# The last unit's values as 64-row products in two PSUM banks, in a transformer block on one core

## The chip, the cores and the metric

One NeuronCore of a Trainium2 chip. The metric is the device time of one execution in microseconds (us); the kernel before took 1579.61 us, the median of three runs (1579.14, 1579.61, 1584.3).

## What is computed

```
xn  = layernorm(x)                                   # x: 2048 tokens x 512
q   = xn @ wq  (32 heads of 16);  k = xn @ wk, v = xn @ wv  (one head, shared)
o   = softmax(q k^T / 4) @ v                         # per head, 2048 x 2048
att = o @ wo
h   = xn @ w1 + b1;  act = h * tanh(softplus(h))     # 1792 wide
out = x + att + act @ w2
```

All inputs and the output are float32.

## The kernel before

The tokens are cut into 4 chunks of 512. A **unit** is 4 heads of one chunk, so there are 32 units, numbered 0 to 31; they run one after the other. In a unit PE makes, for each of 16 tiles of 128 keys and each of 4 heads, a score product (L509, `score`): 128 keys x 512 queries into one PSUM bank. ACT takes the exponential out of PSUM into a tile `pt`, of one bank (L945, 128x512) or of two neighbouring banks at once (L937, 128x1024). When all four heads of a key tile are there, `values` (L511 to L519; its matmul is L513) multiplies them with V: 128 keys x 32 columns, 16 of which are v and 16 ones, which give the softmax's denominators. Head h goes to the partitions 32h to 32h+31 of bank 7, and the 16 key tiles of a unit are added up there. I call the four products of one key tile **a V**. They are full float32, and each matmul leaves two records in the trace, so a V has 8. After the 16th V `attended` (L523) copies bank 7 with ACT to a tile `ov` (L525); for the units 0 to 30 it is stored and gathered back in another layout, for the last unit it stays.

Other products fill PE between scores: the hidden layer (`h..`), the second matrix (`y..`) and the attention's output (`f..`), all at L880. Scores, maxima and these fillers use 64 rows of the array: the upper or the lower half. I call the halves **lanes**; lane 0 is rows 0 to 63, lane 1 rows 64 to 127, and two products in the two lanes run side by side, in different banks. A filler product is split into a lane-0 and a lane-1 part that add into the same bank.

The order of all this is a string, `PLAN`, that is read letter by letter (from L978), and the digit behind a letter names the bank. What the letters in this case mean:

- `e`/`E`: a score in lane 0/1, then its exponential; `f`/`F`: the first score of a wide exponential, whose second score is the next `e` or `E` and takes the next bank. Digit: bank; then a digit or letter for the slot of `pt`.
- `h`/`H`: half a filler product in lane 0/1. The first half of a product is followed by its bank.
- `V`: the next V. `Z`: ACT (or DVE) empties a finished filler product out of its bank (L890 for `y`).
- `|`: PE drains. `G`, `O`, `Q`, `R`, `T` start loads or steps of the output's attention part.

Every engine runs its own instructions in this order, and an instruction waits by semaphore for what it reads and for its bank to be free. So PE's queue stands still behind a score whose bank ACT is still reading. Up to unit 30 the stage also takes the row maxima of the next unit (`s`/`S`, L450, read by DVE at L462); in unit 31 there is none, and DVE has nothing to do. The banks 0 to 6 hold scores and fillers, bank 7 the values.

Behind the last V stands `last_quotient` (L560 to L586). PE first makes 18 products of the output (`last_sums(0, 2)`, L595, with all 128 rows and columns). Then two products with a selection matrix `pick` take the denominators (`pd`, L569) and the values (`po`, L570) out of `ov` into the order that is needed. ACT takes a logarithm and an exponential of `pd` (L574, L575), DVE finishes the quotient (L576 to L578), it is split in two parts (L581, L582), while PE makes 18 more products (`last_sums(2, NT)`); the last 12 products need the quotient. DVE adds each 128-token result to what was there (L585) and SP stores it.

Of the kernel before, what the change touches and what calls it, by code (L numbers as in the profile page):

```python
# [17 lines left out]
P = 128  # L18
# [5 lines left out]
KT = S // P  # L24
KC = S // CT
HG = 4
NU = NC * H // HG
# [132 lines left out]
    "3HhHE6iHhhE2pHs4hOE5ohHHHhe6mS3s2ZVe4nS6E5gE3hNhhChS0e2ahE4bS6hhS5hhhE0eZS3VS6f4cEs2e3fE0mVh1e6aS2e4gS5E3nVE0bs6"  # L160
    "He2cHs3MHe4fHe5hs0HHHs6He2ks3VQF4is6eS0E2ls3Vs6Hf4oS0Es2Ve3aS6H0e4bhS5E2ihHHhs3e6kHS4he5dHhs2HE3chHHs6hRF4ehHes3"
    "S2ZVE6js3e4lE5gGS1hH2HhhHs6hE3hhHs4HE1mhe5nAHhHhS6hE3oZS4s1VHs6E3pf4aeHJE0ce1iTVAP6VVE3dF4eeH6hHHF0gheHHhhe3jHhH"
    "HhhF4kehGHhf0mEVZDVE3if4aeF0ohEGe2hhVVOH3e0gf4cEHe2aHhhCHhHf0ehHEHHHhhhZF4keVf0iH6EhhhhHhHE2bHf4mEHHhhF0ohheZE2h"
    "VVe4gF0ceE5af2eEVGVF0ieF4keVf2mGEH0HHe1bHhhhhhhZHF4oHef2cEVH1e6aHHHf4gEhhhf2eHHhEQhVE6ihf4kEZf2mEVVf4oEH6HHE0jhH"
    "hhhhhZHf2aHeGF4ceRVVF0eeF2ghhEf4kEVF0mehhhf2iEhZVVVTO"
)
PIECES = (
# [11 lines left out]
def attention_and_mlp(ctx: ExitStack, tc: tile.TileContext, x, wq, wk, wv, wo, w1, b1, w2, out):  # L179
    nc = tc.nc  # L180
    E = mybir.EngineType
    PE, SP = nc.tensor, nc.sync
    ACT, DVE, POOL = nc.scalar, nc.vector, nc.gpsimd
# [176 lines left out]
    V = const.tile([P, KT, 2 * DH], F32, name="V")  # L360
# [137 lines left out]
    PT = {}  # L498
# [11 lines left out]

    def values(u, kt):  # L511
        for h in range(HG):
            PE.matmul(  # L513
                BANK[7][h * 32 : (h + 1) * 32],
                V[:, kt],
                PT.pop((u * KT + kt) * HG + h),
                start=kt == 0,
                stop=kt == KT - 1,
            )  # L519

    OD, OHL = {}, {}

    def attended(u):  # L523
        ov = OV[u % 2]
        ACT.activation(ov, BANK[7], AF.Copy)  # L525
        if u == NU - 1:
            return
        j, g = divmod(u, 2)
        if g == 0:
            OD[j] = scratch.tile([2, P, CT], F32, tag="o", name=f"o{u}_dram", bufs=NU // 2)  # L530
        SP.dma_start(out=OD[j][g], in_=ov)
# [28 lines left out]
    def last_quotient():  # L560

        c, mt = NC - 1, DT - 1
        rows = slice(64, P)
        pick = late_pool.tile([P, 2, HG * DH], F32, name="pick")
        DVE.tensor_copy(pick.rearrange("p k (h d) -> p k h d", h=HG), ident.rearrange("p (h k d) -> p k h d", h=HG, k=2))
        po, pd = (BANK[4 + k][rows] for k in range(2))
        ov = OV[(NU - 1) % 2]
        last_sums(0, 2)
        PE.matmul(pd, pick[:, 1], ov, start=True, stop=True)  # L569
        PE.matmul(po, pick[:, 0], ov, start=True, stop=True)  # L570
        last_sums(2, NT)
        hi, lo = (OHL[c, mt][rows, k] for k in range(2))
        o, d, r, z = oc[rows], dc[rows], r0[rows], z0[rows]
        ACT.activation(z, pd, AF.Ln)  # L574
        ACT.activation(r, z, AF.Exp, scale=-1.0)  # L575
        DVE.tensor_tensor(out=d, in0=pd, in1=r, op=ALU.mult)  # L576
        DVE.scalar_tensor_tensor(out=r, in0=d, scalar=2.0, in1=r, op0=ALU.subtract, op1=ALU.mult)
        DVE.scalar_tensor_tensor(out=o, in0=po, scalar=-1.0, in1=r, op0=ALU.mult, op1=ALU.mult)  # L578
        for t in range(NT):
            q = slice(t * P, (t + 1) * P)  # L580
            ACT.activation(hi[:, q], o[:, q], AF.Copy)  # L581
            DVE.tensor_tensor(out=lo[:, q], in0=o[:, q], in1=hi[:, q].bitcast(F32), op=ALU.subtract)  # L582
        for t in range(NT):
            last_products(t, mt)
            DVE.tensor_tensor(out=YS[t], in0=BANK[t], in1=YS[t], op=ALU.add)  # L585
            SP.dma_start(out=of[c * CT + t * P : c * CT + (t + 1) * P, :], in_=YS[t])  # L586

    def last_sums(t0, t1):
        for t in range(t0, t1):
            for mt in range(DT - 1):  # L590
                last_products(t, mt)

    def last_products(t, mt):
        for k, (i, j) in enumerate(TERMS):
            PE.matmul(  # L595
                BANK[t],
                OHL[NC - 1, mt][:, i, t * P : (t + 1) * P],
                RG[(blocks_of[NC - 1, "wo"] + mt) % RING][:, j],
                start=mt == 0 and k == 0,
                stop=mt == DT - 1 and k == 2,  # L600
            )
# [228 lines left out]
    def tiles(n, shape, name, dtype=F32):  # L830
        return [late_pool.tile(shape, dtype, name=f"{name}{i}") for i in range(n)]

    banks = late_ps.tile([P, 8, CT], F32, name="banks")
    BANK = [banks[:, i] for i in range(8)]
# [5 lines left out]
    TY, OV = tiles(2, [P, D], "ty"), tiles(2, [P, CT], "ov")  # L840
# [60 lines left out]
    for p in todo + [None]:  # L901
        c, kind, i, t = (NC - 1, "f", 0, 0) if p is None else (p.c, p.kind, p.i, p.t)
# [74 lines left out]
    for token in word:  # L977
        k = count.get(token, 0)  # L978
# [10 lines left out]
        elif token == "|":  # L989
            PE.drain()  # L990
        elif token == "V":
            values(*divmod(k, KT))
        elif token == "P":
            sent[0] = place_maxima(k, bank=BANK[digit()])
        elif token == "D":
            sent[0]()
        elif token == "Z":
            ended.pop(0).end()
        elif token == "U":
            exponential(k)  # L1000
        elif token == "N":
            ACT.activation(tz, TN[k % 2], AF.Ln, bias=2.0)
        elif token == "M":
            inverse(k)
        elif token == "A":
            hidden_tile(k)
        elif token == "B":
            split_block()
        elif token == "K":
            store_block()  # L1010
        elif token == "W":
            request("w1", k % FT, WB[k % BLOCKS])
        elif token == "G":
            request(*blocks[k], RG[k % RING])
        elif token == "L":
            LOADS[k]()
        elif token == "X":
            reload(k)
        elif token == "J":
            SP.dma_start(**dict(zip(("out", "in_"), outgoing.pop(0))))  # L1020
        else:
            {"O": attended, "C": collect, "Q": logarithm, "R": divide, "T": attention}[token](k)
    last_quotient()


# [26 lines left out]
```

## Time and profile before

| | us |
|---|---|
| median of three runs | 1579.61 |
| the profiled execution | 1579.41 |
| its span, first to last instruction | 1577.3 |
| PE busy | 1554.8 (99%) |
| DVE busy | 1344.5 (85%) |
| ACT busy | 1343.3 (85%) |
| POOL busy | 862.6 (55%) |
| first V of unit 31 starts | 1529.75 |
| its last V is done, the tail's products start | 1560.23 |

Times inside the span count from the first instruction. A row of the timeline has the start, the length, the engine, the source line, the operation, output and inputs, the shape, and the number of instructions that it merges; in brackets the idle time ahead of it and what ended it. "64*128" is the part of the array that is used: 64 rows, 128 columns. A row that merges several is as long as from the first's start to the last's end.

### The profile page before, as it was taken

Reading aid. Unit: us, or ns where it says so; the run is one execution under the profiler, and the core shown is the slowest. Engines: PE = TensorE matmul, PEld = TensorE weight load, DVE = VectorE, ACT = ScalarE, POOL = GpSimd, SP = SyncE. Lnnn points to the kernel's source line nnn. Section 1 sums busy time; section 2 is a strip of 40 time slices with the busy share of each in tenths; the row PEclk is TensorE's granted clock in tenths of the full one; section 3 lists DMA queues with packets and bytes.
Section 4 is the critical chain, followed back from the end, with each engine's and each line's share of the span. In section 5 each row is a group of like instructions: output and inputs, shape, how many; then the busy total and the mean of one; then the engine's idle time right before and its main releaser. Section 6 shows DMA issues by size and latency. Waiting matters only on the chain.

```text
span 1577.3 us, 30275 instructions
## 1 busy us (share of the span) xinstructions
PE 1554.8 (99%) x11589; PEld 855.3 (54%) x11589; DVE 1344.5 (85%) x2215; ACT 1343.3 (85%) x2394; POOL 862.6 (55%) x749
## 2 busy tenths in 40 slices
PE   8989999999999999999999999999999999999999
PEld 6565554555555555555555555555555555555554
DVE  8819999898899889999898999898988898999841
ACT  5548988999899889898899898898888888888996
POOL 5845765587377455643365664452465563543652
PEclk9999999999999999999999999999999999999999
DMA  6682332123233212024223202223231212221130
GB/s 189 250 304 65 131 92 91 60 87 124 84 119 91 85 43 88 29 86 161 98 80 110 101 13 93 70 64 133 90 111 53 93 45 84 85 98 64 62 95 34
DMA packets 66966, 152.00 MB, mean 96 GB/s; under 512 B 9446, under 2 KB 19750, under 8 KB 66438
## 3 DMA queue, kind: packets, MB, share of 16 engines
q1 hardware_dynamic: 66758, 150.06, 28.4%
q8 instruction: 91, 1.49, 0.4%
q14 instruction: 53, 0.43, 0.1%
q10 hardware_dynamic: 64, 0.02, 0.0%
HBM read 97.98 MB, written 51.12 MB: 95 GB/s over the span
## 4 chain that ended last, share of the span: by engine, by line
PE 95%; DVE 2%; ACT 1%; DMA 1%; POOL 1%; issue 0%; SPq 0%; POOLq 0%; ACTq 0%; DVEq 0%
PE banks L513 32%; PE banks L880 23%; PE banks L509 18%; PE banks L450 17%; PE q L656 2%; DVE nm L467 1%; PE banks L595 1%; PE kv L372 0%; PE banks L481 0%; DVE st L304 0%; PE s L450 0%; DVE xs L326 0%; POOL q L412 0%; DMA QS<-mhl 0%; DMA w_dram<-wblk 0%
## 5 line engine op out<-in xcount | busy, mean ns | idle before, releaser
L462 DVE TENSOR_REDUCE nm<-banks 128x1 f32<-128x512 f32 x1984 | 1243.2, 683 | 160.0 <-PE banks L450 110.7
L945 ACT ACTIVATE pt<-banks 128x512 f32<-128x512 f32 x1608 | 867.3, 604 | 119.3 <-PE banks L509 52.7
L450 PE MATMUL banks<-KS,QS 48*128 48x512 f32 x1984 | 680.8, 422 | 6.5 <-ACT pt L945 5.7
L509 PE MATMUL banks<-QS,KS 64*128 64x512 f32 x2048 | 681.8, 419 | 1.1 <-DMA QS<-mhl 1.0
L513 PE MATMUL banks<-pt,V 128*32 128x512 f32 x4096 | 536.4, 603 | 0.0
L509 PEld LDWEIGHTS banks<-QS,KS 64*128 64x128 f32 x2048 | 329.9, 185 | 223.6 <-DVE nm L462 102.4
L450 PEld LDWEIGHTS banks<-KS,QS 48*128 48x128 f32 x1984 | 327.4, 185 | 203.6 <-DVE nm L462 97.7
L880 PE MATMUL banks<-X,wblk 64*128 64x512 f32 x1296 | 333.0, 398 | 0.3
L880 PE MATMUL banks<-ring,act 64*128 64x512 f32 x1344 | 333.1, 397 | 0.1
L937 ACT ACTIVATE pt<-banks 128x1024 f32<-128x1024 f32 x220 | 223.9, 1027 | 39.3 <-PE banks L509 28.3
L880 PEld LDWEIGHTS banks<-X,wblk 64*128 64x128 f32 x1296 | 214.6, 186 | 30.6 <-issue 10.7
L880 PEld LDWEIGHTS banks<-ring,act 64*128 64x128 f32 x1344 | 214.1, 185 | 31.5 <-issue 8.9
L891 POOL TENSOR_TENSOR ysb<-ysb,ty 128x512 f32<-128x512 f32 x80 | 102.7, 1284 | 177.3 <-ACT ty L890 177.2
L513 PEld LDWEIGHTS banks<-pt,V 128*32 128x32 f32 x4096 | 85.5, 108 | 171.4 <-issue 159.5
L636 POOL TENSOR_TENSOR tn<-tn,tr 128x512 f32<-128x512 f32 x54 | 69.5, 1288 | 176.2 <-ACT tr L955 176.0
L950 POOL TENSOR_SCALAR tu<-tu 128x512 f32<-128x512 f32 x54 | 80.2, 1486 | 96.1 <-ACT tu L949 96.0
L235 POOL TENSOR_TENSOR act<-th,act 128x512 fp32r<-128x512 f32 x56 | 72.0, 1287 | 104.6 <-ACT act L234 88.9
L639 POOL TENSOR_TENSOR th<-th,tn 128x512 f32<-128x512 f32 x56 | 72.1, 1288 | 0.0
L638 POOL TENSOR_TENSOR tz<-tz,tn 128x512 f32<-128x512 f32 x54 | 69.6, 1290 | 4.5
L952 POOL TENSOR_TENSOR tn<-tn,tu 128x512 f32<-128x512 f32 x54 | 69.5, 1287 | 4.5
L640 POOL TENSOR_TENSOR th<-th,tz 128x512 f32<-128x512 f32 x54 | 69.6, 1288 | 4.2
L880 PE MATMUL banks<-ring,ohl 64*128 64x512 f32 x288 | 64.5, 395 | 0.0
(113 smaller groups left out, 985.7 us busy)
## 6 DMA issues: line engine op xcount, KB each, us to landing
wblk<-w_dram SPq DMA_DIRECT2D x42, 512.0 KB
ring<-w_dram SPq DMA_DIRECT2D x42, 512.0 KB
QS<-q_dram SPq DMA_DIRECT2D x62, 192.0 KB
q_dram<-q SPq DMA_DIRECT2D x16, 512.0 KB
o_dram<-ov SPq DMA_DIRECT2D x31, 256.0 KB
raw_w<-in_B_w_dram SPq DMA_DIRECT2D x28, 256.0 KB
w_dram<-wblk SPq DMA_DIRECT2D x14, 512.0 KB
w_dram<-ring SPq DMA_DIRECT2D x14, 512.0 KB
```

The source lines that it names most:

```text
L235: POOL.tensor_tensor(out=lo, in0=src, in1=hi.bitcast(F32), op=ALU.subtract)
L450: PE.matmul(tile, QS[u][rows, pair, qt * P : (qt + 1) * P], KS[rows, kc * CT : (kc + 1) * CT], start=True, stop=True,)
L462: DVE.tensor_reduce(out=m[:, a : a + 1], in_=tile, axis=AX.X, op=ALU.max)
L509: PE.matmul(bank, KS[rows, kt * P : (kt + 1) * P], QS[u][rows, pair], start=True, stop=True)
L513: PE.matmul(BANK[7][h * 32 : (h + 1) * 32], V[:, kt], PT.pop((u * KT + kt) * HG + h), start=kt == 0, stop=kt == KT - 1,)
L638: POOL.tensor_tensor(out=z, in0=z, in1=n, op=ALU.subtract)
L639: POOL.tensor_tensor(out=h, in0=h, in1=n, op=ALU.mult)
L880: PE.matmul(self.p, w[rows], x[rows], start=self.first, stop=not any(self.todo))
L891: POOL.tensor_tensor(out=YS[t], in0=YS[t], in1=ty, op=ALU.add)
L937: ACT.activation(slots[slot // 2], banks[:, bank : bank + 2], AF.Exp, scale=SCALE)
L945: ACT.activation(PT[n], BANK[bank], AF.Exp, scale=SCALE)
L950: POOL.tensor_scalar_min(tu, tu, U_MAX)
```

## The change

In the last unit a V is made of eight products: for each head one of the upper 64 keys into bank 7 and one of the lower 64 keys into bank 6. Bank 6 is no longer there for scores and fillers from the first V of unit 31 on: the string's letters stay as they were, its bank digits are new, and one drain `|` is added. Bank 6 is copied by DVE to the other `ov`, and each of the two selecting sums becomes two products that add the two tiles.

```diff
-"...F4keVf0iH6EhhhhHhHE2bHf4mEHHhhF0ohheZE2h"
-"VVe4gF0ceE5af2eEVGVF0ieF4keVf2mGEH0HHe1bHhhhhhhhZHF4oHef2cEVH1e6aHHHf4gEhhhf2eHHhEQhVE6ihf4kEZf2mEVVf4oEH6HHE0jhH"
-"hhhhhZHf2aHeGF4ceRVVF0eeF2ghhEf4kEVF0mehhhf2iEhZVVVTO"
+"...F4keVf0iH2E|hhhhHhHE4bHf0mEHHhhF4ohheZE0"
+"hVVe1gF4ceE3af0eEVGVF4ieF0keVf4mGEH3HHe0bHhhhhhhhZHF4oHef0cEVH2e4aHHHf0gEhhhf4eHHhEQhVE0ihf4kEZf0mEVVf4oEH3HHE0jh"
+"HhhhhhZHf4aHeGF0ceRVVF4eeF0ghhEf4kEVF0mehhhf4iEhZVVVTO"
...
     def values(u, kt):
         for h in range(HG):
-            PE.matmul(
-                BANK[7][h * 32 : (h + 1) * 32],
-                V[:, kt],
-                PT.pop((u * KT + kt) * HG + h),
-                start=kt == 0,
-                stop=kt == KT - 1,
-            )
+            p = PT.pop((u * KT + kt) * HG + h)
+            for bank, rows in ((7, slice(0, P)),) if u + 1 < NU else ((7, slice(0, 64)), (6, slice(64, P))):
+                PE.matmul(
+                    BANK[bank][h * 32 : (h + 1) * 32], V[rows, kt], p[rows], start=kt == 0, stop=kt == KT - 1
+                )
...
         ACT.activation(ov, BANK[7], AF.Copy)
         if u == NU - 1:
+            DVE.tensor_copy(OV[(u + 1) % 2], BANK[6])
             return
...
-        ov = OV[(NU - 1) % 2]
         last_sums(0, 2)
-        PE.matmul(pd, pick[:, 1], ov, start=True, stop=True)
-        PE.matmul(po, pick[:, 0], ov, start=True, stop=True)
+        for out, k in ((pd, 1), (po, 0)):
+            for i in range(2):
+                PE.matmul(out, pick[:, k], OV[i], start=i == 0, stop=i == 1)
         last_sums(2, NT)
```

On PE at the first V of unit 31 (`F4keVf0iH...` in the string; L509 scores, L513 values, L880 a filler of the second matrix; "waits" names the engines whose semaphores the instruction waits for), before:

```order
L509 MATMUL banks<-QS_77,KS 128x512
L513 MATMUL banks<-pt_1112,V 32x512
L513 MATMUL banks<-pt_1119,V 32x512
L513 MATMUL banks<-pt_1115,V 32x512
L513 MATMUL banks<-pt_1119,V 32x512
L509 MATMUL banks<-QS_77,KS 128x512 [waits Activation_49]
L880 MATMUL banks<-ring_1120,act_1131 128x512 [waits DMAHW5_49,Activation_49]
```

and in the change, where lines behind L519 have moved and L515 is the matmul of `values`, L879 that of the fillers:

```order
L509 MATMUL banks<-QS_77,KS 128x512
L515 MATMUL banks<-pt_1112,V 32x512
L515 MATMUL banks<-pt_1112,V 32x512 [waits Activation_49]
L515 MATMUL banks<-pt_1119,V 32x512 x2
L515 MATMUL banks<-pt_1115,V 32x512 x2
L515 MATMUL banks<-pt_1119,V 32x512 x2
L509 MATMUL banks<-QS_77,KS 128x512
L879 MATMUL banks<-ring_1120,act_1131 128x512 [waits DMAHW5_49]
```

Each of the four products has become two, and the wait for ACT that the filler had (it took bank 6 over) has moved ahead into the V, to its first product for bank 6.

On PE in the tail (L595 and L594 the output's products, L569 and L570 the selecting ones), before:

```order
L595 MATMUL banks<-ring_1124,ohl_1137 128x512 x3
L569 MATMUL banks<-ov_1147,pick 64x512 [waits DVE_49,Activation_49]
L570 MATMUL banks<-ov_1147,pick 64x512
L595 MATMUL banks<-ring_1122,ohl_1135 128x512 x3
L595 MATMUL banks<-ring_1123,ohl_1136 128x512 x3
```

and in the change:

```order
L594 MATMUL banks<-ring_1124,ohl_1137 128x512 x3
L569 MATMUL banks<-ov_1146,pick 64x512 [waits DVE_49]
L569 MATMUL banks<-ov_1147,pick 64x512 [waits Activation_49]
L569 MATMUL banks<-ov_1146,pick 64x512
L569 MATMUL banks<-ov_1147,pick 64x512
L594 MATMUL banks<-ring_1122,ohl_1135 128x512 x3
```

Two selecting products have become four, the first and third of them from the tile that DVE writes.

On DVE ahead of the tail (L525 the new copy, L564 and L565 the making of `pick`, L575 and L576 the quotient's first step), before:

```order
L565 COPY pick<-ident 128x128
L576 TENSOR_TENSOR dc_1152<-banks,or_1153 64x512 [waits PE_49,Activation_49,Pool_49]
L577 SCALAR_TENSOR_TENSOR or_1153<-dc_1152,or_1153 64x512 [waits DVE_49,Pool_49]
L578 SCALAR_TENSOR_TENSOR oc_1151<-banks,or_1153 64x512 [waits DVE_49,PE_49,Pool_49]
L582 TENSOR_TENSOR ohl_1133<-oc_1151,ohl_1133 64x128 [waits Activation_49] x4
```

and in the change:

```order
L525 COPY ov_1146<-banks 128x512 [waits DMAHW5_49,PE_49,Activation_49]
L564 COPY pick<-ident 128x128
L575 TENSOR_TENSOR dc_1152<-banks,or_1153 64x512 [waits Activation_49,Pool_49]
L576 SCALAR_TENSOR_TENSOR or_1153<-dc_1152,or_1153 64x512 [waits DVE_49,Pool_49]
L577 SCALAR_TENSOR_TENSOR oc_1151<-banks,or_1153 64x512 [waits DVE_49,PE_49,Pool_49]
```

The making of `pick` now stands behind a copy that waits for the last V.

More of the change, by code (lines that the diff above doesn't have):

```diff
@@ L162 @@
     "S2ZVE6js3e4lE5gGS1hH2HhhHs6hE3hhHs4HE1mhe5nAHhHhS6hE3oZS4s1VHs6E3pf4aeHJE0ce1iTVAP6VVE3dF4eeH6hHHF0gheHHhhe3jHhH"
-    "HhhF4kehGHhf0mEVZDVE3if4aeF0ohEGe2hhVVOH3e0gf4cEHe2aHhhCHhHf0ehHEHHHhhhZF4keVf0iH6EhhhhHhHE2bHf4mEHHhhF0ohheZE2h"
-    "VVe4gF0ceE5af2eEVGVF0ieF4keVf2mGEH0HHe1bHhhhhhhZHF4oHef2cEVH1e6aHHHf4gEhhhf2eHHhEQhVE6ihf4kEZf2mEVVf4oEH6HHE0jhH"
-    "hhhhhZHf2aHeGF4ceRVVF0eeF2ghhEf4kEVF0mehhhf2iEhZVVVTO"
+    "HhhF4kehGHhf0mEVZDVE3if4aeF0ohEGe2hhVVOH3e0gf4cEHe2aHhhCHhHf0ehHEHHHhhhZF4keVf0iH2E|hhhhHhHE4bHf0mEHHhhF4ohheZE0"
+    "hVVe1gF4ceE3af0eEVGVF4ieF0keVf4mGEH3HHe0bHhhhhhhZHF4oHef0cEVH2e4aHHHf0gEhhhf4eHHhEQhVE0ihf4kEZf0mEVVf4oEH3HHE0jh"
+    "HhhhhhZHf4aHeGF0ceRVVF4eeF0ghhEf4kEVF0mehhhf4iEhZVVVTO"
 )
```

## The prediction, made before the change ran

> **What bounds the kernel now.** I read the page first, its chain second, and then only the stretch that the change touches. The profiled execution took 1579.41 us with a span of 1577.3; the difference of 2.1 us lies around the span and I leave it as it is.
>
> ```profile
> span 1577.3 us, 30275 instructions
> PE 1554.8 (99%) x11589; PEld 855.3 (54%) x11589; DVE 1344.5 (85%) x2215; ACT 1343.3 (85%) x2394; POOL 862.6 (55%) x749
> PE 95%; DVE 2%; ACT 1%; DMA 1%; POOL 1%; issue 0%; SPq 0%; POOLq 0%; ACTq 0%; DVEq 0%
> ```
>
> Over the whole span PE is the bound. But that is an average over 32 units, and the edit touches the last one, which is a different stage: there are no maxima left to take. The stretch from the first values of unit 31 (1529.7) to the last (1560.2), in windows and then in groups:
>
> ```profile
> 1529.70:1540.00 10.30, 10.30 (x85) 4.53 (x83) 0.00 (x0) 10.14 (x15) 2.56 (x2) 1.00 0.56 178
> 1540.00:1550.00 10.00, 10.00 (x82) 5.10 (x80) 0.00 (x0) 10.00 (x14) 1.91 (x2) 1.00 0.01 2
> 1550.00:1560.30 10.30, 10.30 (x82) 4.71 (x79) 0.00 (x0) 10.02 (x14) 7.07 (x7) 1.00 0.01 2
> ```
>
> ```profile
> L937 ACT ACTIVATE pt<-banks 128x1024 f32<-128x1024 f32 x24 | 23.4, 1044 | 0.0
> L513 PE MATMUL banks<-pt,V 128*32 128x512 f32 x128 | 15.8, 600 | 0.0
> L509 PE MATMUL banks<-QS,KS 64*128 64x512 f32 x54 | 13.3, 422 | 0.0
> L880 PE MATMUL banks<-ring,act 64*128 64x512 f32 x57 | 10.8, 399 | 0.0
> ```
>
> The columns of a window are its length, then busy time and count of PE, PEld, DVE, ACT and POOL, the granted clock, and DMA. DVE does nothing here; PE and ACT are both full (10.30 and 10.14, 10.00 and 10.00, 10.30 and 10.02). A busy PE is modelled, so I ask ACT what it waited for in this stretch, and look at its last chain of exponentials:
>
> ```profile
> ACT pt L945 <- PE banks L509: 0.2, 1, 0.2
> ```
>
> ```profile
> 1554.37 4.69 ACT L937 ACTIVATE pt<-banks 128x1024 f32<-128x1024 f32 x5
> 1558.90 0.65 ACT L890 ACTIVATE ty<-banks 128x512 f32<-128x512 f32 x1
> ```
>
> Five wide exponentials take 1558.90 - 1554.37 = 4.53 us, 0.906 each, and ACT waits once, for 0.2 us, in 30 us. **ACT is the bound of the last unit**: a PE that is faster there gains at most those few tenths; a PE that is later than ACT's queue of ready scores costs its full lateness.
>
> How much slack has PE? Its rows there:
>
> ```profile
> 1529.75 1.07 PE L513 MATMUL banks<-pt,V 128*32 128x512 f32 x8
> 1530.75 0.50 PE L509 MATMUL banks<-QS,KS 64*128 64x512 f32 x1
> 1533.30 0.50 PE L509 MATMUL banks<-QS,KS 64*128 64x512 f32 x2
> 1533.72 1.92 PE L513 MATMUL banks<-pt,V 128*32 128x512 f32 x16
> 1535.58 0.96 PE L509 MATMUL banks<-QS,KS 64*128 64x512 f32 x6
> ```
>
> One V (one key tile of values, 8 records) holds PE from 1529.75 to 1530.75, 1.00 us, and two hold it from 1533.72 to 1535.58, 1.86. So a V takes 0.86 and a run of them 0.14 more to leave. Entering costs about 0.1 (the second of two scores in 1533.30 to 1533.80 starts at 1533.41, being 0.39 long, and the run at 1533.72, where a lane steps by 0.23: the 30 products at 1566.42 below are 7.13 long), and the second pair of scores behind a run comes 0.1 late too: some 0.34 per run. The 16 V lie in 10 runs. PE's need is 16 x 0.86 + 10 x 0.34 + (54 + 57)/2 x 0.23 = 13.8 + 3.4 + 12.8 = 30.0 of 30.5 us. It has half a microsecond of slack. Both engines are full, and the banks between them are what lets one run ahead of the other.
>
> **The tail behind the last V.**
>
> ```profile
> 1557.52 2.78 PE L513 MATMUL banks<-pt,V 128*32 128x512 f32 x24
> 1560.23 4.39 PE L595 MATMUL banks<-ring,ohl 128*128 128x512 f32 x18
> 1560.37 0.60 ACT L525 ACTIVATE ov<-banks 128x512 f32<-128x512 f32 x1 [0.35 <-PE banks L513]
> 1564.56 1.07 PE L569 MATMUL banks<-ov,pick 128*64 128x512 f32 x2
> 1565.46 1.02 PE L570 MATMUL banks<-ov,pick 128*64 128x512 f32 x2
> 1565.66 0.59 ACT L574 ACTIVATE oz<-banks 64x512 f32<-64x512 f32 x1 [4.70 <-PE banks L569]
> 1566.42 7.13 PE L595 MATMUL banks<-ring,ohl 128*128 128x512 f32 x30
> 1569.70 0.91 DVE L582 TENSOR_TENSOR ohl<-oc,ohl 64x128 fp32r<-64x128 f32 x4 [0.37 <-ACT ohl L581]
> 1571.55 2.80 DVE L585 TENSOR_TENSOR ysb<-banks,ysb 128x512 f32<-128x512 f32 x4 [0.94 <-PE banks L595]
> ```
>
> PE runs without a break from 1557.52 to 1573.55: three V, 18 products, two selecting products, 30 products.
>
> **The change part by part.** (1) *Two more selecting products.* Each is two records; the two of before stand 1564.56 to 1566.42 with the switch, 0.86 to 0.9 us each without it. Two more are +1.7 us of PE. Is there cover? The logarithm needs both products of pd, so it starts 0.86 later; the quotient's first piece (DVE 1569.70 + about 0.25) then comes at about 1570.8. PE reaches the product that needs it 18 x 0.23 behind 1566.42 + 1.7, at about 1572.3. PE is still the later one, so all of it counts: **+1.7**.
>
> (2) *Bank 6 copied by DVE, and pick behind it on DVE.* DVE's 128x512 adds in the last row take 0.7 each; the copy and the small copy of pick end near 1561.5, beside the 18 products that run to 1564.56. Nothing; without that cover it would be some 0.7.
>
> (3) *The first V needs bank 6 empty.* Before, V only needs bank 7.
>
> ```profile
> 1530.17 0.65 ACT L890 ACTIVATE ty<-banks 128x512 f32<-128x512 f32 x1
> 1530.64 2.02 ACT L937 ACTIVATE pt<-banks 128x1024 f32<-128x1024 f32 x2
> 1530.87 0.61 PE L880 MATMUL banks<-ring,act 64*128 64x512 f32 x2
> 1531.20 0.39 PE L509 MATMUL banks<-QS,KS 64*128 64x512 f32 x1
> ```
>
> Bank 6 holds a product that ACT empties at 1530.17 to 1530.82, and the product that reuses it starts at 1530.87. Now the second matmul of the first V waits there, and all of PE's queue behind it: the run moves from 1529.75 to 1530.87, 1.1 us. Behind it stand the two scores (1530.75 and 1531.20) that ACT's second wide exponential at about 1531.63 reads the moment they are done (1531.20 + 0.39). No slack: **+1.1**. It could be less, down to nothing, only if that exponential had its scores from ahead of the V; the order of the tokens is unchanged, so it has not.
>
> (4) *Six banks for the rest.* One bank of the six holds an open product, so the scores go round in two pairs, where they had three. I compared every score of the new digits with the time at which ACT ended the reading of its bank in the trace of before. 13 scores, or first scores of a pair, come too early, by 0.1 to 0.9 us, 6.1 us in all; 8 of the 9 later V runs have one or more just ahead of them. The first and the last of the 13, from PE's side:
>
> ```profile
> 1532.24 0.52 PE L509 MATMUL banks<-QS,KS 64*128 64x512 f32 x2
> 1556.37 0.50 PE L509 MATMUL banks<-QS,KS 64*128 64x512 f32 x1
> ```
>
> At 1532.24 the new digits name the pair that the second exponential of the row at 1530.64 reads to its end at 1532.66 (0.4 late); at 1556.37 the pair of the third of the five from 1554.37, to 1557.23 (0.9 late). One worked out, the place `E6i h f4k E Z f2m E VV`, now `E0i h f4k E Z f0m E VV`:
>
> ```profile
> 1546.59 0.49 PE L509 MATMUL banks<-QS,KS 64*128 64x512 f32 x1
> 1546.92 0.63 PE L509 MATMUL banks<-QS,KS 64*128 64x512 f32 x4
> 1547.31 0.60 ACT L945 ACTIVATE pt<-banks 128x512 f32<-128x512 f32 x1
> 1547.48 1.92 PE L513 MATMUL banks<-pt,V 128*32 128x512 f32 x16
> 1549.16 1.96 ACT L937 ACTIVATE pt<-banks 128x1024 f32<-128x1024 f32 x2
> 1549.34 0.50 PE L509 MATMUL banks<-QS,KS 64*128 64x512 f32 x2
> ```
>
> f2m went at about 1547.16 into a free pair. f0m needs bank 0, which E0i filled just before and whose exponential ends at 1547.91: 0.8 late, and the two V behind it too. The scores at 1549.34 come at about 1550.14 and are done 0.5 later, at 1550.6; ACT wants them at 1549.16 + 0.91 = 1550.07. So 0.8 us of PE wait became a stall of about 0.55: ACT's queue covers a third. Two thirds of 6.1 are **+4.1**. The ends: 6.7 if nothing is covered (each release adds 0.05), 2.0 if PE regains time where ACT itself was late. I take the middle because the worked place is of the common size.
>
> (5) *The values as eight products of 64 rows.* The trace has no 64-row product with 32 columns. The bounds: 0.86 a V if eight tiles run side by side as four do, 1.72 if the two row tiles take turns, so 0 to 13.8 us. The nearest rows are the pairs of 64-row scores, of which six run in 0.96 us (1535.58), two lanes at once; I take 0. Eight weight loads take 0.16 us, so sixteen fit below 0.86:
>
> ```profile
> 1551.95 0.16 PEld L513 LDWEIGHTS banks<-pt,V 128*32 128x32 f32 x8 [0.35 <-issue]
> ```
>
> Does the switch of 0.34 a run go, now that rows are split in two everywhere? The last run leaves to L595, from 128x32 to 128x128: the row split does not change, only the columns, and yet 1560.23 - 1557.52 = 2.71 is three V and the same 0.14. So a change of columns alone pays, and 64x128 to 64x32 is one: I keep it, between 0 and -3.4 of PE time. The Trainium skill, "TensorEngine Tiling (Array Packing)", Key Properties, says the same: changing the tiling mode, not just the tile, drains TensorE, and it lists 64x128 and 64x32 as two modes. The trace agrees (0.14); by the rule the sum stays, without it rival A below holds.
>
> (6) *One drain more.* At most a run's 0.34; nothing in the sum, since ACT has just been made late there.
>
> Sum: 1.7 + 1.1 + 4.1 = +6.9 on 1579.41, **1586.3 us**. The profiled execution stands 0.2 under the median of the runs (1579.61), so the change should be read as +0.43%.
>
> **Rivals.** *A, not slower:* the switches do go, since no product spans both row tiles any more and each lane moves on by itself. PE regains 10 x 0.34 = 3.4 us just where it is late, and 4.1 falls to 0.7: 1.7 + 1.1 + 0.7 = +3.5, 1582.9, within 0.3% of before. It decides where the gap behind a run falls below 0.05. Against it: the 0.14 at 1560.23. It cannot become faster: ACT's gaps are 0.2 us and the tail alone adds 1.7. *B, the eight products don't do what they say:* the row tiles take turns in full fp32. A V takes 1.72, PE is the bound, 13.8 - 0.5 of slack + 1.7 + 1.1, the waits for banks then hidden: +16.1, 1595.5. For it: no such product in the trace; against it the score pairs. In the Trainium skill, "TensorE: Matmul & The Clock Gate", Measured speedup vs the span model, each further tile adds about 4 ns; no run here shows it for these products, and it would leave the sum as it is.
>
> **How the numbers follow.** A measurement of this kernel can tell 0.3%, 4.7 us, from no change. The forecast has 0.66, with 1.7 + 1.1 + (2.0 to 6.7), 1584.2 to 1588.9; A 0.18; B 0.15; faster, by something that I don't see, 0.01. The range takes in A and the forecast's upper end with some slowness of the values, 1582.0 to 1590.5, and leaves out B and a little below. Slower: the forecast and B, less its lowest edge, 0.80; same 0.19; faster 0.01.
>
> **What would show it.** Four records each for the two selecting sums, and 1.7 us more between the last V and the last DVE add. The first V of unit 31 beginning its second half behind ACT's L890 eviction, and about 1 us of ACT idle behind it. ACT waiting for scores some 5 us in all in the last unit, in pieces of 0.2 to 0.8, instead of 0.2. A V run of one from start to next score still 1.00. It is wrong if a V takes other than 0.86 (rival B, or something between), if the gap behind runs vanishes (A), or if ACT's waits stay below 2 us.

## The result and the profile after

The changed kernel takes 1591.74 us (median of 16 executions, 1587.69 to 1596.73). The kernel before takes 1583.74 us in the same comparison (16 executions, 1579.14 to 1588.10). The ratio is 1.0047, with a 95% interval of 1.0033 to 1.0061: 7.4 us slower, between 5.2 and 9.7; the two medians lie 8.0 apart. The forecast of +0.43% holds as a difference; the forecast time of 1586.3 us, with its range to 1590.5, does not hold, mainly because the executions of before that it started from lie 4 us under the median of sixteen.

The page of the changed kernel, its span and its busy times:

```profile
span 1589.8 us, 30539 instructions
PE 1565.4 (98%) x11721; PEld 859.9 (54%) x11721; DVE 1346.6 (85%) x2216; ACT 1345.1 (85%) x2394; POOL 862.1 (54%) x749
```

The profiled execution took 1591.93 us, 12.5 us more than that of before. Three differences add up to it. The stretch ahead of the first V of unit 31 is 4.1 us longer (that V starts at 1533.86, before at 1529.75), although the code there is the same. From the first V to the first product of the tail I call **R**, and from there to the end of the span **T**. In windows, first of the changed kernel, then of before (length; busy time and count of PE, PEld, DVE, ACT, POOL; granted clock; DMA):

```profile
1533.86:1571.06 37.20, 35.58 (x367) 15.97 (x365) 0.00 (x0) 31.42 (x41) 12.03 (x10) 1.00 0.15 51
1571.06:1589.80 18.74, 14.98 (x64) 9.87 (x56) 6.88 (x13) 2.72 (x7) 1.33 (x2) 0.98 0.15 56
```

```profile
1529.75:1560.23 30.48, 30.48 (x239) 14.27 (x237) 0.00 (x0) 30.11 (x41) 11.47 (x10) 1.00 0.20 62
1560.23:1577.30 17.07, 13.32 (x56) 9.32 (x52) 5.72 (x11) 2.72 (x7) 1.93 (x2) 1.00 0.16 61
```

R grows by 6.72 and T by 1.66 (to the exact ends of the spans): **8.4 us** come from the change, against 6.9 forecast. R is where both engines were full. Now ACT, with the same 41 instructions, is idle for 37.20 - 31.42 = 5.8 us, before for 0.4, and its busy time has itself grown by 1.3. Both together are the 6.72. The 1.3 is a thing to see in such a row: wide exponentials that follow one another overlap (0.906 from start to start, 1.02 to 1.03 long behind a pause), so every break in ACT's queue costs some 0.12 on top of the idle time.

What ACT waited for in R, in the changed kernel (us in total, times, longest):

```profile
ACT pt L936 <- PE banks L509: 2.9, 6, 0.9
ACT pt L944 <- PE banks L509: 1.3, 2, 0.8
ACT ty L889 <- PE banks L879: 0.6, 1, 0.6
```

4.8 us of waits for PE stand where there were 0.2; "some 5" was forecast. The first of them is the wait for bank 6. The timeline of the changed kernel at the first V, in PE's and ACT's rows:

```profile
1533.86 2.20 PE L515 MATMUL banks<-pt,V 64*32 64x512 f32 x16
1534.28 0.65 ACT L889 ACTIVATE ty<-banks 128x512 f32<-128x512 f32 x1
1534.76 1.09 ACT L936 ACTIVATE pt<-banks 128x1024 f32<-128x1024 f32 x1
1534.98 0.18 PEld L515 LDWEIGHTS banks<-pt,V 64*32 64x32 f32 x14 [0.98 <-ACT ty L889]
1536.00 0.49 PE L509 MATMUL banks<-QS,KS 64*128 64x512 f32 x1
1536.34 0.39 PE L509 MATMUL banks<-QS,KS 64*128 64x512 f32 x1
1536.77 1.03 ACT L936 ACTIVATE pt<-banks 128x1024 f32<-128x1024 f32 x1 [0.92 <-PE banks L509]
```

The V starts with its half in bank 7 and stands until ACT has emptied bank 6 (1534.93); the other 14 weight loads follow at 1534.98. The next score comes 2.14 us behind the V's start, where it came 1.00 behind it. ACT has finished its wide exponential at 1535.85 and waits 0.92 for the two scores.

The place that the prediction worked out (`E0i h f4k E Z f0m E VV f4oE`), again in the changed kernel:

```profile
1556.20 0.60 ACT L944 ACTIVATE pt<-banks 128x512 f32<-128x512 f32 x1
1556.85 0.50 PE L509 MATMUL banks<-QS,KS 64*128 64x512 f32 x2 [0.45 <-ACT pt L944]
1557.28 1.95 PE L515 MATMUL banks<-pt,V 64*32 64x512 f32 x32
1558.08 1.05 ACT L936 ACTIVATE pt<-banks 128x1024 f32<-128x1024 f32 x1
1559.16 0.50 PE L509 MATMUL banks<-QS,KS 64*128 64x512 f32 x2
1559.77 1.03 ACT L936 ACTIVATE pt<-banks 128x1024 f32<-128x1024 f32 x1 [0.64 <-PE banks L509]
```

The pair of scores at 1556.85 waits 0.45 for the exponential that empties bank 0 (to 1556.80), the two V stand behind it, the scores behind them come at 1559.16, and ACT is idle for 0.64. Forecast were 0.8 and 0.55: PE waited less than forecast and ACT more, so nothing of the wait was covered here.

A run of one V and its next product:

```profile
1550.65 1.09 PE L515 MATMUL banks<-pt,V 64*32 64x512 f32 x16
1551.67 0.49 PE L879 MATMUL banks<-ring,act 64*128 64x512 f32 x1
```

1.02 us, before 1.00; two V take 1.88 (1557.28 to 1559.16), before 1.86. Sixteen records in the time of eight: the two row tiles run side by side, and the switch to the next product is still paid (1.02 for one V that takes 0.86 inside a run).

The tail:

```profile
1571.06 4.38 PE L594 MATMUL banks<-ring,ohl 128*128 128x512 f32 x18
1571.32 0.69 DVE L525 COPY ov<-banks 128x512 f32<-128x512 f32 x1 [50.20 <-PE banks L515]
1571.93 0.54 DVE L564 COPY pick<-ident 128x128 f32<-128x128 f32 x1
1575.38 3.65 PE L569 MATMUL banks<-ov,pick 128*64 128x512 f32 x8
1578.95 7.09 PE L594 MATMUL banks<-ring,ohl 128*128 128x512 f32 x30
```

The selecting products hold PE from 1575.38 to 1578.95, 3.57 us, where they held it for 1.86: 1.71 more. DVE's two copies end at 1572.47, far ahead of 1575.38, and PE makes its last 30 products in 7.09 us without a break (before 7.13), so it doesn't wait for the quotient.

### The profile page after: what moved, and what is told of

It is laid out like the page before. It is cut to its first block, busy times and chain, and to the rows that moved or that the text cites. A ratio compares the mean times of both kernels' runs of the same rounds, so it can differ in the third digit from the quotient of the medians.

```text
span 1589.8 us, 30539 instructions
## 1 busy us (share of the span) xinstructions
PE 1565.4 (98%) x11721; PEld 859.9 (54%) x11721; DVE 1346.6 (85%) x2216; ACT 1345.1 (85%) x2394; POOL 862.1 (54%) x749
## 4 chain that ended last, share of the span: by engine, by line
PE 92%; DVE 2%; DMA 2%; ACT 1%; POOL 1%; issue 0%; SPq 0%; POOLq 0%; ACTq 0%; DVEq 0%
PE banks L515 31%; PE banks L879 22%; PE banks L509 18%; PE banks L450 17%; PE q L655 2%; DVE nm L467 1%; PE banks L594 1%; DMA QS<-q_dram 1%; PE kv L372 0%; DVE st L304 0%; DMA ring<-w_dram 0%; PE banks L481 0%; DMA o_dram<-ov 0%; PE s L450 0%; DVE xs L326 0%
## 5 line engine op out<-in xcount | busy, mean ns | idle before, releaser
L450 PE MATMUL banks<-KS,QS 48*128 48x512 f32 x1984 | 682.2, 423 | 6.9 <-ACT pt L944 5.9
L509 PE MATMUL banks<-QS,KS 64*128 64x512 f32 x2048 | 685.2, 420 | 2.6 <-DMA QS<-mhl 1.0
L515 PE MATMUL banks<-pt,V 128*32 128x512 f32 (+1 forms) x4224 | 538.6, 604 | 0.1
L509 PEld LDWEIGHTS banks<-QS,KS 64*128 64x128 f32 x2048 | 330.8, 185 | 227.1 <-DVE nm L462 102.4
L450 PEld LDWEIGHTS banks<-KS,QS 48*128 48x128 f32 x1984 | 328.1, 185 | 205.3 <-DVE nm L462 97.1
L879 PE MATMUL banks<-ring,act 64*128 64x512 f32 x1344 | 335.4, 398 | 0.5 <-DMA ring<-w_dram 0.3
L879 PE MATMUL banks<-X,wblk 64*128 64x512 f32 x1296 | 334.3, 399 | 0.3
L879 PEld LDWEIGHTS banks<-ring,act 64*128 64x128 f32 x1344 | 214.9, 185 | 32.6 <-issue 9.5
L879 PEld LDWEIGHTS banks<-X,wblk 64*128 64x128 f32 x1296 | 215.5, 187 | 31.4 <-issue 11.1
L515 PEld LDWEIGHTS banks<-pt,V 128*32 128x32 f32 (+1 forms) x4224 | 86.2, 108 | 171.8 <-issue 159.3
L879 PE MATMUL banks<-ring,ohl 64*128 64x512 f32 x288 | 64.4, 395 | 0.0
```

The lines of the kernel that those rows point to most:

```text
L450: PE.matmul(tile, QS[u][rows, pair, qt * P : (qt + 1) * P], KS[rows, kc * CT : (kc + 1) * CT], start=True, stop=True,)
L509: PE.matmul(bank, KS[rows, kt * P : (kt + 1) * P], QS[u][rows, pair], start=True, stop=True)
L515: PE.matmul(BANK[bank][h * 32 : (h + 1) * 32], V[rows, kt], p[rows], start=kt == 0, stop=kt == KT - 1)
L879: PE.matmul(self.p, w[rows], x[rows], start=self.first, stop=not any(self.todo))
```

## The experiments

R and T are read in each kernel's own trace, so what happened ahead of unit 31 does not enter; equal code gives equal values (R 30.48 and 30.46, 37.20 and 37.21; T 18.77 and 18.77 in pairs of kernels that differ elsewhere). Whole times stand beside them as ratios to the kernel before on the same chip. A single execution's time carries no argument: it moves by some 4 to 5 us with the granted clock (the share of PE's full clock that the profile shows as granted), as shown further below.

**The digits alone.** The kernel before with the string of the change; values, copy and selecting products as before.

```diff
-"...f0iH6EhhhhHhHE2bHf4mEHHhhF0ohheZE2h"
+"...f0iH2E|hhhhHhHE4bHf0mEHHhhF4ohheZE0"
...
```

> The kernel before with the bank digits and the drain of the change alone: values stay products of 128 rows into bank 7, bank 6 is merely unused in the last unit. Measured in each run's own profile as R, from the first V of unit 31 to the first product of the tail (before 30.48 us, change 37.20), and T, from there to the end of the span (before 17.07, change 18.74). Theory (the banks cost, the 64-row products don't): the first V has no wait for bank 6 any more, all else of the loss stays: R 36.2, T 17.1, in all +5.7 us or +0.36%. Rival (the eight 64-row products are what cost, by their own time or their starts): R below 32, in all below +1.5 us.

The window of R, and ACT's waits in it:

```profile
1532.52:1568.42 35.90, 34.35 (x240) 15.22 (x238) 0.00 (x0) 31.29 (x41) 12.02 (x10) 1.00 0.15 52
```

```profile
ACT pt L937 <- PE banks L509: 1.9, 5, 0.6
ACT pt L945 <- PE banks L509: 0.7, 1, 0.7
ACT ty L890 <- PE banks L880: 0.6, 1, 0.6
ACT pt L945 <- PE banks L880: 0.5, 1, 0.5
```

1589.13 us, ratio 1.0041 (1.0027 to 1.0056); T is 17.08, as before (17.10 to the exact end of its span). R is 35.90, where the theory had 36.2 and the rival less than 32; ACT waits 3.7 us for PE: 5.4 of the 6.7 us come from the six banks and the drain, without any 64-row product and without a second bank of values.

**Four selecting products alone.** The kernel before, with DVE copying the ready tile to the other `ov`; the sums take both tiles, so the two outputs are the double of before.

```diff
+            DVE.tensor_copy(OV[(u + 1) % 2], ov)
...
-        PE.matmul(pd, pick[:, 1], ov, start=True, stop=True)
-        PE.matmul(po, pick[:, 0], ov, start=True, stop=True)
+        for out, k in ((pd, 1), (po, 0)):
+            for i in range(2):
+                PE.matmul(out, pick[:, k], OV[i], start=i == 0, stop=i == 1)
```

> The kernel before with four selecting products in place of two: DVE copies ov, and each sum adds both copies; both sums are doubled, so their quotient is the same. Theory (PE is unbroken in the tail): T 17.07 + 2 x 0.86 = 18.8, R unchanged at 30.5, +0.11%. Rival (only the denominators' second product counts, the other lies beside the quotient): T 17.9, +0.05%.

R 30.46, T 18.77; 1585.65 us, ratio 1.0020 (1.0006 to 1.0033). T has grown by 1.67 (from 17.10, to the exact ends of the spans), all that the change adds there, as the theory had it.

**The change with the two banks added by DVE.** DVE adds bank 6 to `ov` instead of copying it, and two selecting products suffice.

```diff
-            DVE.tensor_copy(OV[(u + 1) % 2], BANK[6])
+            DVE.tensor_tensor(out=ov, in0=BANK[6], in1=ov, op=ALU.add)
...
-            for i in range(2):
-                PE.matmul(out, pick[:, k], OV[i], start=i == 0, stop=i == 1)
+            PE.matmul(out, pick[:, k], OV[(NU - 1) % 2], start=True, stop=True)
```

> The change, but DVE adds bank 6 to the copy of bank 7 (ov), and the two selecting products of before are back. Theory: copy and add take some 1.5 us behind the last V, beside the 18 products that take 4.3: T 17.1, R unchanged at 37.2, 1.7 us less than the change. Rival (the longer way of copy, add and selection reaches the path): T 18 or more.

R 37.21, T 17.08: T is that of before again, since the sum on DVE (0.69 us) lies beside the 18 products. 1589.49 us, ratio 1.0052 (1.0031 to 1.0072). So the tail's 1.67 was avoidable, and R does not hang on it.

**The first V later.** The change with the first V of unit 31 behind the product that takes bank 6's place, where bank 6 is empty without a wait.

```diff
-"...F4keVf0iH2E|hhhhHhHE4b..."
+"...F4kef0iH2E|hhhhHhVHE4b..."
```

> The change with the first V of unit 31 moved nine letters back in the string, behind the scores and fillers that it held up; by then bank 6 is empty. R is counted from where the first V would have stood, the end of the scores ahead of it plus 0.3 us. Theory (the wait for bank 6 costs its full length once): ACT's idle time of 0.9 us behind it goes, R 36.2. Rival (the wait only takes the place of later waits for banks, since ACT frees them no earlier): R stays within 0.3 of 37.2.

The rival's case came: PE no longer waits for bank 6, but ACT does not gain. Rows of the new place:

```profile
1538.34 1.09 PE L515 MATMUL banks<-pt,V 64*32 64x512 f32 x16
1539.36 0.50 PE L879 MATMUL banks<-ring,act 64*128 64x512 f32 x1
1540.12 0.60 ACT L944 ACTIVATE pt<-banks 128x512 f32<-128x512 f32 x1 [1.70 <-PE banks L509]
```

ACT is idle for 1.70 us in one piece, where the change had 0.92 and 0.57. With R counted from the last maxima product (15.78 us ahead of the first V in the change), it is 37.3 instead of 37.2. 1595.43 us, ratio 1.0084 (1.0067 to 1.0100): some 5 us more than R and T explain (2 to 7 by the interval). Two readings take most of it away. All six executions have a mean granted clock of 0.991 to 0.993; the nine executions of the kernel before with 0.990 to 0.992 have a median of 1585.01, which is 10.4 less, against 8.5 by R and T. And the profiled execution leaves nothing over: it took 14.2 us more than that of before, of which 5.8 lie ahead of the edit, in the same code (the last maxima product starts at 1519.76, before at 1513.97, in the change at 1518.08), 6.8 between there and the tail, and 1.6 in the tail. Whether the edit has a part in the remaining 2 us of the medians stays open.

**Less work for ACT, before and after.** DVE has nothing to do in unit 31, so it takes over ACT's evictions of the `y` products there (and POOL's adding of them), in the kernel before and in the change; the third kernel has the DVE sum of the third experiment as well.

```diff
+            elif self.kind == "y" and reduced[NU - 1] == HG * KT:
+                DVE.tensor_tensor(out=YS[t], in0=self.p, in1=YS[t], op=ALU.add)
```

> The kernel before, with the fillers of the last unit emptied by DVE (which adds them to their sum itself) instead of by ACT and POOL: six evictions of 0.48 us leave ACT. Theory (ACT is the bound of the last unit, PE is full too with some half a microsecond to spare): R falls from 30.5 to about 30.0, T stays 17.1; -0.5 us, at most -0.03%. Rival (PE's fullness is only modelled, ACT alone is the bound): R falls by the whole 2.9 us to 27.6, -0.18%.

> The change with the same evictions by DVE. Theory (banks come free too late and PE stands still ahead of V runs): ACT has 2.9 us less and frees its banks sooner after each eviction, bank 6 is empty 0.5 us sooner for the first V; but ACT is idle 5 us here, waiting for scores, so only part comes through: R from 37.2 to 35.5 to 36.5. Rival (ACT's own work is the bound in the change too): R falls by 2.9 or more, to 34.3.

> The change with DVE's evictions and with DVE adding the two tiles, so that two selecting products are enough: the two cheap repairs together. Theory: they add up, R as in the run with the evictions alone, T 17.1, still 5 us behind the kernel before. Rival (with the repairs the 64-row products pay, because the switches are gone): R at or under 30.5.

The kernel before with this edit, R and ACT's waits:

```profile
1530.55:1561.00 30.45, 30.45 (x240) 13.92 (x238) 4.99 (x7) 27.97 (x35) 4.83 (x5) 1.00 0.21 62
```

```profile
ACT pt L939 <- PE banks L509: 1.1, 4, 0.5
ACT pt L947 <- PE banks L509: 0.7, 1, 0.7
```

ACT has 6 instructions less, its busy time falls by 2.1, and R stays (30.45 for 30.48): the time saved comes back as waits for PE. The theory had 30.0, the rival 27.6: so PE seems to have less to spare than even the theory said. 1583.18 us, ratio 1.0005 (0.9989 to 1.0022). In the change R falls from 37.20 to 36.57 and 36.55, a little less than expected, while ACT's waits rise from 4.8 to 6.4 us; ratios 1.0057 (1.0035 to 1.0079) and 1.0040 (1.0023 to 1.0058), T 18.69 and 17.00. Neither rival came. After the change ACT is not short of time, it is short of scores.

**The drain alone.** The kernel before with nothing but the added `|`.

```diff
-"...f0iH6Ehhhh..."
+"...f0iH6E|hhhh..."
```

> The kernel before with one more drain of PE at the place where the change has it (behind the first scores of unit 31), and nothing else. Theory (the drain is none of the loss; it is the digits): R within 0.3 of 30.5. Rival (the drain holds PE's queue until both lanes have run dry, with the fillers behind it): R 31 or more, a part of the 5.4 us that the digits and the drain cost together.

PE's rows around it, the same place in the kernel before (its second score started at 1531.20), and the window of R with the drain:

```profile
1532.99 0.38 PE L509 MATMUL banks<-QS,KS 64*128 64x512 f32 x1
1533.48 0.95 PE L880 MATMUL banks<-ring,act 64*128 64x512 f32 x5
1534.15 0.39 PE L509 MATMUL banks<-QS,KS 64*128 64x512 f32 x1
```

```profile
1531.32 0.84 PE L880 MATMUL banks<-ring,act 64*128 64x512 f32 x5
1531.90 0.39 PE L509 MATMUL banks<-QS,KS 64*128 64x512 f32 x1
```

```profile
1531.53:1562.72 31.19, 31.08 (x239) 14.34 (x237) 0.00 (x0) 30.25 (x41) 11.47 (x10) 1.00 0.20 60
```

R is 31.19, 0.71 more than before; the whole time can't show it (1583.01 us, ratio 0.9997, 0.9985 to 1.0008). The fillers in the other lane start 0.49 behind the start of the second score, that is after its end (1533.37); before they started 0.12 behind it, beside it. The next score comes 1.16 behind that start; before it came 0.70 behind. So the drain delays both lanes by some 0.4 to 0.5, and in a stage without slack that and a little more reached the end: the rival's case. The changed kernel, behind its second score at 1536.34, shows the same:

```profile
1537.52 0.39 PE L509 MATMUL banks<-QS,KS 64*128 64x512 f32 x1
1538.37 0.60 ACT L944 ACTIVATE pt<-banks 128x512 f32<-128x512 f32 x1 [0.57 <-PE banks L509]
```

The next score comes 1.18 behind, and ACT, which has just been late by 0.92, is idle for another 0.57. The digits without the drain were not run, so what the drain costs inside the change is read from these rows and not measured.

**Less work for PE.** The kernel before with two thirds of the half products of the last four `y` tiles left out (32 products; their sums lack these terms), alone and together with the DVE edit above.

```diff
+            if self.light and n % 3:
+                return
+            w, x = self.products[n]
```

> The kernel before with 32 half products of fillers left out in the last unit (the two correction terms of the last four tiles of the second matrix): PE has 3.7 us less to do there, ACT the same. Theory now (both engines bound the last unit, neither has slack): ACT's work holds R, which falls only by ACT's idle time of 0.3 to 0.8, to 29.7 to 30.2. Rival (after the evictions by DVE gained nothing: PE alone is the bound): R falls by 3.7, to 26.8.

> The same 32 half products left out and the evictions by DVE as well: each of the two engines has about 3 to 3.7 us less. Theory (both bound it): now R falls by most of the smaller relief, 2.9, to between 27.5 and 28.5, although the evictions alone gave nothing. Rival (the exponentials' order and the banks bound it, not the engines' work): R stays above 29.5.

The windows of R, one fence for each kernel:

```profile
1532.63:1562.81 30.18, 29.44 (x207) 10.87 (x205) 0.00 (x0) 30.00 (x41) 11.33 (x10) 1.00 0.18 62
```

```profile
1529.93:1559.21 29.28, 28.83 (x208) 10.93 (x206) 4.23 (x7) 27.59 (x35) 4.76 (x5) 1.00 0.20 64
```

With less PE work ACT never waits for it, and R falls by 0.3 only, to ACT's own time. With less of both it falls by 1.2. Relief of one engine alone gains 0.03 or 0.3, of both 1.2: the engines hold R together. How much further it could fall is not told by this: 29.28 lies between what theory and rival expected. (1582.06 and 1578.35 us, single executions at mean granted clocks of 0.992 and 0.993, with before at 1584.81 and 0.992 beside them.)

**The digits with V moved.** The first kernel of this series (digits alone), with V runs put ahead of the score that waits for its bank, or behind the next one.

```diff
-"...ZE0hVVe1g...f0eEVGVF4ieF0keVf4mGE...Zf0mEVVf4oE...F0ghhEf4kEVF0me..."
+"...ZVVE0he1g...VGVf0eEF4ieVF0kef4mGE...ZVVf0mEf4oE...F0ghhEVf4kEF0me..."
```

> The run with the digits alone, with the V runs at six places moved ahead of the score that waits for its bank in front of them, so that PE works off values while ACT reads the bank. Theory (two pairs of banks hold 0.9 us of work for ACT, a V run of 1.0 or 1.9 us is longer, whatever its place): the idle time moves from behind the run to behind the swapped score, R between 35.2 and 36.5 (35.9 without the move). Rival (only the order of the letters was left unfit for six banks): each place gives back some 0.6, R 33.5 or less.

```profile
ACT pt L936 <- PE banks L508: 1.2, 4, 0.6
ACT ty L889 <- PE banks L879: 1.0, 2, 0.6
ACT pt L944 <- PE banks L508: 0.7, 1, 0.7
ACT pt L944 <- PE banks L879: 0.5, 1, 0.5
```

R is 35.51, for 35.90: the waits stay (3.4 us for 3.7), at other places. At these places, too, two pairs of banks do not carry ACT over a V run. (1584.99 us, one execution at 0.994, before 1584.81 at 0.992.)

**Two banks without 64-row products.** The digits alone, and heads 2 and 3 of the last unit into bank 6 with all 128 rows: the wait for bank 6 is there, the row split is not. ACT copies the upper 64 partitions from bank 7, DVE the lower 64 from bank 6, and two selecting products suffice.

```diff
-                BANK[7][h * 32 : (h + 1) * 32],
+                BANK[7 if u + 1 < NU or h < 2 else 6][h * 32 : (h + 1) * 32],
...
+            ACT.activation(ov[:64], BANK[7][:64], AF.Copy)
+            DVE.tensor_copy(ov[64:], BANK[6][64:])
```

> The digits and the drain of the change with values of 128 rows, four products a V, but heads 2 and 3 of the last unit go to bank 6 in place of bank 7 (ACT copies one half, DVE the other, into one ov; two selecting products). So the first V waits for bank 6 as in the change, and no product is split by rows. Theory (the eight 64-row products cost nothing by themselves, the wait for bank 6 makes the whole 1.3 us between the digits alone, 35.9, and the change, 37.2): R 37.0 to 37.3, T 17.1. Rival (the split costs that 1.3 us, the wait is hidden by later waits for banks): R 35.9 to 36.2.

PE's rows at the first V:

```profile
1535.27 2.17 PE L513 MATMUL banks<-pt,V 128*32 128x512 f32 x8
1537.37 0.50 PE L509 MATMUL banks<-QS,KS 64*128 64x512 f32 x1
```

The score comes 2.10 us behind the start of the V, for 1.00 with the digits alone, and R goes from 35.90 to 36.99: +1.09. ACT waits 4.6 us. What is left to the change's 37.20, 0.2, is all that the row split can have cost. T is 17.09. (1591.43 us, one execution at 0.992, before 1580.8 at 0.994.)

## Why the difference was near and the time wrong

The terms, each with the pair of kernels that isolates it, R and T of one trace each:

| term of the sum | forecast | measured | from |
|---|---|---|---|
| two more selecting products | +1.7 | +1.67 | T of before and with the four products alone |
| the first V waits for bank 6 | +1.1 | +1.09 | R of the digits alone and with heads in two banks |
| six banks | +4.1 | +4.71 | R with the drain alone and with the digits |
| drain | 0 | +0.71 | R of before and with the drain alone |
| eight 64-row products | 0 | +0.21 | R with heads in two banks and of the change |
| DVE's copy | 0 | 0 | ends at 1572.47, needed at 1575.38 |
| sum | +6.9 | +8.4 | |

The terms of R are a chain of kernels, each with one part more, so they add up to the difference by construction; in another order the drain and the six banks might share their 5.4 differently. Each R and T is of one trace; where code is equal they agree within 0.02 (R) and some 0.1 (T).

**The step that failed** is the last of the sum, its base: "The profiled execution stands 0.2 under the median of the runs (1579.61), so the change should be read as +0.43%", and the 1586.3 was made on 1579.41. The sum had no term for how far one execution of the same code stands from the next, and the median of three was 4.1 us under the median of sixteen. The change's +6.9 on 1583.74 gives 1590.6, the measured 8.4 gives 1592.1, for 1591.74. So 4.3 us of the 5.4 by which the time was missed are the base (1583.74 for 1579.41); the rest are the terms, which the traces show 1.5 too small. That +0.43% came so near to the measured +0.47% is in part luck: by the terms of the traces, 8.4 us, it should have been +0.53%. The row of three times (1579.14, 1579.61, 1584.3) already showed 5 us between neighbours.

Where does such a difference arise? The executions fall into two groups by the mean granted clock of each. Of the sixteen of the changed kernel, the seven at 0.994 to 0.995 took 1587.69 to 1589.08 us, the nine at 0.990 to 0.992 took 1591.56 to 1596.73. Of the seventeen of the kernel before that stand beside the first four experiments, the eight at 0.994 to 0.996 took 1579.93 to 1581.47, the nine at 0.990 to 0.992 took 1582.72 to 1587.14. The execution that the forecast was made on has 0.995. Within a group the medians of the changed kernel (1588.45 and 1593.68) lie 8.1 and 8.7 us above those of before (1580.38 and 1585.01), close to the 8.4 of the traces. The chip of the sixteen is not on record, so this pairing may join two chips.

In the traces the maxima products (L450) of the changed kernel run 0.4 us ahead of those of before up to 108 us, and 2.9 behind at 154; between 697 and 740 us 0.8 is added, between 1286 and 1333 0.6. The windows of 120 to 140 us and of 121 to 128, first both of the change and then both of before:

```profile
120.00:140.00 20.00, 19.78 (x115) 9.08 (x115) 16.66 (x28) 13.84 (x25) 7.04 (x6) 0.80 0.11 40
121.00:128.00 7.00, 6.89 (x29) 3.22 (x29) 4.25 (x7) 3.27 (x6) 1.27 (x1) 0.50 0.00 0
```

```profile
120.00:140.00 20.00, 19.78 (x137) 10.15 (x136) 19.54 (x33) 16.90 (x31) 9.71 (x8) 0.98 0.20 65
121.00:128.00 7.00, 6.78 (x48) 3.20 (x46) 6.54 (x12) 5.84 (x11) 1.30 (x1) 1.00 0.00 0
```

The granted clock (the last column but two) is 0.80 against 0.98 over the 20 us, and PE gets 115 matmuls done in place of 137, in code that is the same. All fourteen kernels' traces have a stretch at half the clock there, around a pause of PE of 5.6 to 6.1 us that ends at 115.89 in the kernel before and at 115.65 in the change. What differs is its length: by the clock records of the traces it lasts 10.2 us in seven of them (110.7 to 121.0 in the kernel before) and 13.7 or 17.1 us in the other seven (111.1 to 128.1 in the change). Kernels with old and with new digits are in both groups. The first V of unit 31 starts at 1532.63 to 1536.96 where the stretch is long (without the kernel that moves it), at 1529.75 to 1532.52 where it is short. That goes with the clock; what makes the full clock return sooner in one execution than in another is not shown, and no edit here tested it.

The other steps. **ACT and PE as joint bounds** held: relief of one engine gained 0.03 or 0.3, of both 1.2. The half microsecond of slack that PE was given was, if anything, too much, since taking 2.1 us of work from ACT gained 0.03. **The bank-6 wait** held in place, size and effect; the later V shows that moving the V by nine letters does not get rid of it. **Six banks**: the mechanism held, the size was 0.6 too small. The list of 13 late scores, 6.1 us, left out narrow ones: the same comparison finds three more, at 1533.40, 1540.32 and 1543.51, late by 0.66, 0.54 and 0.21, so 7.5 us in 16 scores. In the changed kernel these three (1539.93, 1548.37, 1551.92) do start 0.05 behind the end of the exponential that reads their bank. Of 7.5 us 4.71 came through, so "ACT's queue covers a third" was about right over all, though in the worked place it covered nothing; two thirds of 7.5 would have been 5.0. **The drain** is the one term of the sum that was wrong in kind: I took "at most a run's 0.34; nothing in the sum, since ACT has just been made late there", and it cost 0.71 in the kernel before, where ACT had not been made late. The drain also empties the other lane, and in the change's own rows ACT's second pause, 0.57, stands right behind it: being late by 0.92 just before did not cover it. **The 64-row products** held: a run of one takes 1.02 for 1.00, a run of two 1.88 for 1.86; ten runs with 0.02 more are the 0.2 of the table. **Rival A** (the switches go) is out: the gap behind a run is where it was, so the row split does not do away with the switch. **Rival B** (the row tiles take turns) is out by the same rows: 1.72 a V would make a run of two 3.4 long.

No kernel here that does the whole work beats the one before beyond what the measurement tells. The quickest form of the whole change, with the sum and the evictions on DVE, is still 0.4% slower (0.23 to 0.58).

## What to carry to other kernels

Count PSUM banks as the length of the queue between two full engines. Here, while ACT reads one of two pairs only the other can be ready, 0.9 us of work for it, and a run of one or two V with the two scores behind it takes PE 1.5 to 2.4 us (1.02 or 1.88, and 0.5). Taking one bank away cost 4.7 us in this order of the work; moving the V runs gave back 0.4 and relieving ACT 0.6, and the 64-row products brought nothing to set against it. Relieving PE in the changed kernel, or spreading its work over the six banks in another way, was not tried, so 4.7 is the price of this string of digits and not of six banks as such. Ask of a bank that changes its owner who empties it last, and what stands in the in-order queue behind the first instruction that needs it. Make the sum as a difference, and before putting it on an absolute time ask how far two executions of the same code lie apart, and which clock the one at hand was granted.

## What the runs showed of the hardware

- Eight full-float32 products of 64 rows and 32 columns, in two row tiles and four column tiles, take the time of four with 128 rows: 0.86 a V between V of one run (1.02 for one, 1.88 for two).
- Leaving 64x32 tiles for 64x128 costs what leaving 128x32 did: from the start of a run to the next product it is 0.02 us more (1.02 for 1.00, 1.88 for 1.86).
- A drain of PE between two half-array lanes cost 0.71 us of a stage of 30.5, where the delay of the next products themselves was 0.4 to 0.5.
- ACT's exponentials overlap in a full queue: wide ones start 0.906 us apart, and one behind a pause takes 1.02 to 1.03.
- In all fourteen profiles the granted clock fell to half around a pause of PE of 5.6 to 6.1 us, beginning between 110 and 117 us; it stayed there for 10.2 us in seven profiles and for 13.7 or 17.1 in seven, in code that is the same.
- Executions of the same kernel differ with their mean granted clock: the changed kernel took at most 1589.08 us at 0.994 to 0.995 and at least 1591.56 at 0.990 to 0.992.
